# A gate moved at the head of the load queue, one pair's x turned by DMA, and the last output tile in two halves

## The chip, the cores and the metric

The kernel runs on one core of a Trainium2 chip, as one launch. The metric is device time in microseconds (us). The engines of the core are named as in the profile: PE is TensorE (PEld its weight loads), DVE is VectorE, ACT is ScalarE, POOL is GpSimd and SP is SyncE. SP computes nothing: it issues DMAs, as POOL and ACT also do.

## The reference

A recurrent attention with a decaying state feeds a two-layer network with a GELU. Inputs and output are float32.

```python
# q, k, v, alpha: (4 batches, 8 heads, 768 tokens, 48)
for t in range(S):
    state = alpha[:, :, t, :, None] * state + np.einsum('bhd,bhe->bhde', k[:, :, t], v[:, :, t])
    y[:, :, t] = np.einsum('bhd,bhde->bhe', q[:, :, t], state)
x = y.transpose(0, 2, 1, 3).reshape(3072, 384)
h = x @ w_in                                     # w_in: (384, 2048)
g = 0.5 * h * (1.0 + np.tanh(np.sqrt(2 / np.pi) * (h + 0.044715 * h * h * h)))
out = g @ w_out                                  # w_out: (2048, 384)
```

## The kernel before, in words

**Tiling.** The 768 tokens are cut into six chunks of 128, and the four batches into two halves of two. A chunk with a half is a *pair*: twelve pairs, number m = 0 to 11, two batches each. A chunk with one batch is a *unit*: 24 units, each giving one output tile of 128 x 384.

**A pair's attention.** ACT takes the logarithm of alpha (`ln`, la), PE sums it along the tokens with a triangular matrix (`cum`), ACT takes exponentials (`b`, `binv`, and `bend` for the chunk's end). DVE multiplies q by b (qp) and k by binv (kp). Both are turned so that features lie on partitions (qkT): for pairs 0 to 7 by PE transposes and copies, for pairs 8 to 11 by a DMA transpose (`turn_dma`, L402). PE multiplies the turned k and q (`at`, L424), DVE masks the result (`atm`, L431), PE multiplies by v and adds the carried state (`yps`, L470 and L473). PE also computes the pair's contribution to the state (`kv`), which DVE carries on (`st`). A copy gives x in bfloat16 (L480, on ACT or DVE).

**Turning x.** The first layer needs x with features on partitions (xT). The pairs in `TURN_X` have it turned by a DMA transpose from SP (`turn_x_dma`, L408), the others by three PE transposes for each unit (xT_ps, L487) and a copy by DVE (L491). Before, `TURN_X` holds pairs 8 to 11.

**The two layers.** For each pair, 16 groups of three matmuls of 256 columns give hT (`layer1`, L497), and ACT applies the GELU into gT (L503). For each unit, 16 matmuls of 384 columns add up acc (`layer2`, L511), in four parts of four; a copy (ot, L518) and a store from SP (L523) follow. Layer 2 of pairs 0 and 1 runs after layer 1 of both, part by part over their four units; from then on each pair's layer 2 follows its layer 1.

**The order.** A planner (`Scheduler.order`) fixes the order of the instructions of every engine when the kernel is built. It goes through the tasks with costs from `W` and takes, on the engine that is free first, the task with the best priority; buffers have to come free first (`BUFS`: four tiles for layer 1's results and acc together, tag "ff"). Layer 1 and layer 2 tasks form a stream in fixed order; where PE would idle, matmuls on zeros ("idle", `fill`, L222) are put in. On the chip each engine then runs its list strictly in that order.

**Loads.** alpha, q and k of pair 0 and alpha and q of pair 1 come in quarters of 96 KB from SP and ACT (`RINGS`). All other loads are issued by POOL in the order of `LOADS`, those that change the type (v, w_in, w_out) among them. w_in and w_out come in four parts each. The entry `gatea0` is a tiny copy on POOL that reads a tile of pair 0, so that everything behind it in POOL's queue waits until that tile has landed:

```python
LOADS = ('gatea0', 'v0', 'pk1', 'in 0', 'in 1', 'v1', 'in 2', 'in 3', 'out 0', 'out 1', '2a', ...)

elif step[:4] == "gate":
    key = step[4], int(step[5]), 3
    gate = [s.add("gate", {"POOL": 150}, n, self.wait(*key), [loads[key]])]
```

'pk1' is k of pair 1 in quarters, 'in 0' a part of w_in, '2a' the first half of pair 2's four inputs, '3' all four of pair 3.

Of the kernel before, what the change touches and what calls it, by code (L numbers as in the profile page):

```python
# [7 lines left out]
F32 = mybir.dt.float32  # L8
# [6 lines left out]
W = dict(  # L15
    ln=760, exp=720, bend=170, gelu4=510, gelu2=340, table=1290,
    cum=530, cum_packed=1500, t8=450, t4=225, attn=340, kv=170, inter=170, intra=205, tx=168, l1_4=655, l1_2=340, l2=655,
    qk2=910, qk1=500, ev8=650, ev4=350, mask=640, st=1400, st0=700, xc=520, xe=330, ot=540,
    ev8_act=960, ev4_act=520, xc_act=450, xe_act=450, ot_act=450,
    strip=2120, cast=1500, weight=2080, dma=2100, issue=1100, wissue=760, sp=100, store=2600, turn=1250, landed=2200, xbar_qk=1500, xbar_x=1000, piece=330, piece_issue=450, begin=2700, cast_0=1300, share=1200, cast_1=1900, ln_packed=1040, cold=380, fill=216, zero=1100,  # L20
)
LAT = {"SP": 0, "PE": 210, "ACT": 110, "DVE": 90, "POOL": 0}

# [113 lines left out]
class _Kernel:  # L137
# [3 lines left out]

    SPLIT = (2,)
    EARLY = (0, 1)
    LOADS = ('gatea0', 'v0', 'pk1', 'in 0', 'in 1', 'v1', 'in 2', 'in 3', 'out 0', 'out 1', '2a', 'out 2', '2b', 'out 3', '3', '4', '5', '6', '7', '8', '9', '10', '11')

    PACKED, CUM_FF, R = (0, 1), (1,), 4
    RINGS = (('a', 0, 0, 'SP'), ('a', 0, 2, 'ACT'), ('a', 0, 1, 'SP'), ('a', 0, 3, 'ACT'), ('q', 0, 0, 'SP'), ('q', 0, 2, 'ACT'), ('q', 0, 1, 'SP'), ('q', 0, 3, 'ACT'), ('k', 0, 0, 'SP'), ('k', 0, 2, 'SP'), ('k', 0, 1, 'SP'), ('k', 0, 3, 'SP'), ('a', 1, 0, 'SP'), ('a', 1, 1, 'SP'), ('a', 1, 2, 'SP'), ('a', 1, 3, 'SP'), ('q', 1, 0, 'SP'), ('q', 1, 1, 'SP'), ('q', 1, 2, 'SP'), ('q', 1, 3, 'SP'))
    TABLE = ('q', 0, 3)

    TURN_QK, TURN_X = (8, 9, 10, 11), (8, 9, 10, 11)  # L150

    EV_ACT = (0, 1, 2, 3)

# [352 lines left out]
    def layer2(self, f, c, b, part):  # L506
        def emit(e):
            if part == 0:
                f["acc", c, b] = self.tile("ff", [self.C, self.d_model], F32, "acc")
            for nt in range(part * 4, part * 4 + 4):  # L510
                self.nc.tensor.matmul(f["acc", c, b], self.gT[c % self.NG][:, nt, b * self.C:(b + 1) * self.C],  # L511
                                      self.w_out[:, nt, :], start=nt == 0, stop=nt == self.NFT - 1)
        return emit

    def result(self, f, c, b):
        def emit(e):
            f["ot", c, b] = self.tile("ot", [self.C, self.d_model], F32)
            self.copy(e)(f["ot", c, b], f.pop(("acc", c, b)))  # L518
        return emit

    def store(self, f, c, b):
        r = b * self.S + c * self.C
        return lambda e: self.nc.sync.dma_start(self.out[r:r + self.C, :], f["ot", c, b])  # L523


    def tasks(self):
        s = self.s = Scheduler(self.BUFS, self.fill, 60000)
        B, NCH = self.B, self.NCH
# [5 lines left out]
        loads, n, gate = {}, 0, []  # L534
# [20 lines left out]
        for r, m, j, e in self.RINGS:  # L555
            loads[r, m, j] = s.add("load", {e: W["piece_issue"]}, n, self.load_packed(r, *pairs[m], j), land=W["piece"] + (0 if n else W["begin"]))
            n += 1
            if (r, m, j) == self.TABLE:
                s.add("table", {"ACT": W["table"]}, n, lambda e: self.act_set(LN_EXP))
        for step in self.LOADS:  # L560
            if step[0] == "v":
                rows(int(step[1:]), "v")
            elif step[0] == "p":
                r, m = step[1], int(step[2])
# [19 lines left out]
        for m, (c, i) in enumerate(pairs):  # L584
            u, P = self.p[c, i], 100 * m
# [5 lines left out]
            for lo, hi in self.parts(m):  # L591
                n = hi - lo
                ln = s.add("ln", {"ACT": W["ln_packed" if u["packed"] else "ln"] * n // 2}, P, self.ln(u, lo, hi), rows_of("a", m, lo), LN_EXP)
                cum = s.add("cum", {"PE": W["cum_packed" if u["packed"] else "cum"] * n // 2}, P - 400, self.cum(u, lo, hi), [ln])
                x = [s.add(e, {"ACT": W[e] if e == "bend" else W["exp"] * n // 2}, P + 2 + j, self.exp(u, e, lo, hi), [cum], LN_EXP)
                     for j, e in enumerate(("b", "binv", "bend") if u["sums"] else ("b", "binv"))]
# [37 lines left out]
            for j in range(2):  # L634
                b, o = 2 * i + j, P + 10 + 3 * j
                k = kp[j]
                if u["packed"]:
                    turned = every
                elif m not in self.TURN_QK:
                    turned = []  # L640
                    for which in ("q", "k") if early else ("qk",):
                        n = 4 * len(which)
                        cost = {"DVE": W[f"ev{n}"]}
                        if m in self.EV_ACT:
                            cost["ACT"] = W[f"ev{n}_act"]
                        t1 = s.add("t", {"PE": W[f"t{n}"]}, o, self.turn(u, j, which),
                                   ([qp[j]] if "q" in which else []) + ([k] if "k" in which else []))
                        turned.append(s.add("ev", cost, o, self.turned(u, j, which), [t1]))
                        t1.take("yk", turned[-1])
                        tq.append(t1)  # L650
                        if len(tq) == 1:
                            owner = turned[0]
                at = s.add("attn", {"PE": W["attn"]}, o + 1, self.attn(u, j), turned)
                ms = [s.add("mask", {"DVE": W["mask"]}, o + 2, self.mask(u, j, h), [at]) for h in range(2)]
                if (m, j) in self.AT_FF:
                    at.take("ff", ms[0]).take("ff", ms[1])
                else:
                    at.take("ca", *ms)
                y = s.add("y", {"PE": W["intra"] + (W["inter"] if c else 0)}, P + 20 + j, self.y(u, j, c, b),
                          ms + turned + [loads["v", m, j]] + ([states[b, c - 1]] if c else []))  # L660
                xc = s.add("x", {"ACT": W["xc_act"], "DVE": W["xc"]}, P + 20 + j, self.x(u, j), [y])
                if m in self.TURN_X:
                    xe = tx = s.add("turn", {"SP": W["turn"]}, P + 22 + j, self.turn_x_dma(u, j, c, b), [xc], xbar=W["xbar_x"])
                else:
                    tx = s.add("tx", {"PE": W["tx"]}, P + 22 + j, self.turn_x(u, j), [xc])
                    xe = s.add("xe", {"DVE": W["xe"]}, P + 22 + j, self.turned_x(u, j, c, b), [tx])
                    tx.take("yk", xe)
                y.take("yk", xc)
                xc.take("x", tx)
                users += [at, y]  # L670
                ats.setdefault(m, []).append(at)
                ms[0].take("atm", y)
                xts[c, b], ys[b, c] = xe, y
                vs.append(y)
                if c < NCH - 1:
                    if u["packed"]:
                        tb = s.add("t", {"PE": W["t4"]}, P + 29 + j, self.turn_back(u, j), turned)
                        k = s.add("ev", {"DVE": W["ev4"], "ACT": W["ev4_act"]}, P + 29 + j, self.turned_back(u, j), [tb])
                        tb.take("yk", k)
                        users.append(tb)  # L680
                        backs.append(tb)
                    kv = s.add("kv", {"PE": W["kv"]}, P + 30 + j, self.kv(u, j), [k, loads["v", m, j]])
                    st = states[b, c] = s.add("st", {"DVE": W["st" if c else "st0"]}, P + 30 + j, self.carry(u, j, c, b),
                                              [kv, be[j]] + ([states[b, c - 1], ys[b, c - 1]] if c else []))
                    kv.take("yk", st)
                    vs.append(kv)
                    kvs.append(kv)
                    cs.append(st)
# [14 lines left out]


        n = 0
        f, gs, l2s = {}, {}, {}
        between = {m: [x for p in self.DECAYS.get(m, ()) for x in ends[p]] for m in range(-1, len(self.BLOCKS))}

        def layer1(m):
# [14 lines left out]
        def layer2(m):  # L724
            nonlocal n
            units = [(pairs[p][0], 2 * pairs[p][1] + j) for p in ((0, 1) if m == 0 else self.BLOCKS[m]) for j in range(2)]
            parts = range(self.NFT // 4)
            first = {}
            for u, part in ([(u, part) for part in parts for u in units] if m == 0 else [(u, part) for u in units for part in parts]):
                c, b = u  # L730
                t = s.add("l2", {"PE": W["l2"]}, 10000 + n, self.layer2(f, c, b, part),
                          gs[m if m else b // 2][4 * part:4 * part + 4] + [loads["w", "out", part]], stream=n)
                l2s.setdefault(c, []).append(t)
                n += 1
                first.setdefault(u, t)
                if part == parts[-1]:
                    ot = s.add("ot", {"DVE": W["ot"], "ACT": W["ot_act"]}, -1, self.result(f, c, b), [t])
                    first[u].take("ff", ot)
                    ot.take("ot", s.add("store", {"SP": W["sp"]}, n, self.store(f, c, b), [ot]))

        for m in range(len(self.BLOCKS)):
            layer1(m)
            if m:
                layer2(m if m > 1 else 0)
# [64 lines left out]
```

## Time and profile before

| | |
|---|---|
| median of 11 runs (range) | 186.93 us (186.58 to 189.28) |
| the profiled execution's own time | 186.84 us |
| its span, first to last instruction | 185.1 us |
| granted PE clock | 1.00 |
| busy: PE, ACT, DVE, POOL | 175.8, 135.3, 105.7, 60.5 us |
| first matmul of layer 1; of layer 2 | 18.62; 33.55 us |
| first layer 1 of pairs 7 and 8 | 122.14; 135.66 us |
| end of the last POOL load | 110.9 us |
| last copy; last store issued; landed | 181.55; 182.06; 183.91 us |

A row of the profile's groups gives the line, the engine, the operation and what it writes and reads, and behind x the number of instructions. "DMA to landing" is the time from the start of an issue until its semaphore says that all has arrived. The chain that ended last is followed back from the last instruction, at each step to what released it. In the lines of slices the span is cut into 40 equal parts of 4.6 us, and each digit is the busy share in tenths.

### The profile page before, as it was taken

What the parts mean: (1) busy time and instruction counts of PE and PEld (TensorE: products, weight loads), DVE (VectorE), ACT (ScalarE), POOL (GpSimd) and SP (SyncE); (2) the same over time, 40 slices, a digit from 0 to 9 for tenths busy, and PEclk for the clock granted to TensorE, in tenths of its full rate; (3) what the DMA queues carried; (4) which work ended last, traced back from release to release, by engine and by line L of the source; (5) the groups of instructions that cost most, each with busy time, mean ns of one, the idle gap of its engine ahead of it and who ended that gap; (6) DMA issues with size and microseconds to landing.
All of it is one profiled execution on the core that took longest, in us unless ns stands there. A gap on an engine that the chain in (4) does not pass through costs nothing.

```text
span 185.1 us, 4604 instructions
## 1 busy us (share of the span) xinstructions
PE 175.8 (95%) x1851; PEld 128.3 (69%) x1851; DVE 105.7 (57%) x235; ACT 135.3 (73%) x308; POOL 60.5 (33%) x67
## 2 busy tenths in 40 slices
PE   7867999999999999999999999999999999999992
PEld 2444878666686787787688778667687677686860
DVE  7774873055969895596499798596644615000000
ACT  3646978873888789869799759788789883491931
POOL 2977356976545755644750200000000000000000
PEclk9999999999999999999999999999999999999999
DMA  5999999999999999999999966154180280311102
GB/s 152 186 222 196 199 232 209 204 208 174 191 276 179 161 231 195 186 223 198 179 227 219 177 177 118 41 122 82 39 179 27 54 189 4 87 46 43 43 7 78
DMA packets 50229, 27.56 MB, mean 149 GB/s; under 512 B 37984, under 2 KB 47264, under 8 KB 50208
## 3 DMA queue, kind: packets, MB, share of 16 engines
q0 software_dynamic: 32096, 17.70, 69.3%
q1 hardware_dynamic: 17536, 9.18, 20.1%
q10 hardware_dynamic: 576, 0.39, 0.7%
q8 instruction: 14, 0.23, 0.6%
q14 instruction: 7, 0.06, 0.1%
HBM read 25.17 MB, written 4.72 MB: 161 GB/s over the span
## 4 chain that ended last, share of the span: by engine, by line
PE 84%; DMA 8%; ACT 3%; SPq 2%; issue 1%; DVE 0%; ACTq 0%; DVEq 0%
PE acc L511 34%; PE hT L497 31%; DMA q<-in_q_dram 6%; PE at L424 4%; PE qkT_ps L364 4%; PE yps L473 2%; PE yps L470 2%; PE cum L320 2%; PE kv L441 2%; SPq L247 2%; DMA qkT<-kp 2%; PE xT_ps L487 1%; ACT L503 1%; ACT ot L518 1%; PE cum L322 1%
## 5 line engine op out<-in xcount | busy, mean ns | idle before, releaser
L497 PE MATMUL hT<-xT,w_in 128*128 128x256 bf16 x576 | 70.5, 273 | 0.6 <-ACT gT L503 0.6
L503 ACT ACTIVATE gT<-hT 128x256 bf16<-128x256 f32 x192 | 63.4, 386 | 8.6 <-PE hT L497 8.0
L511 PE MATMUL acc<-w_out,gT 128*128 128x384 bf16 x384 | 68.9, 326 | 0.0
L497 PEld LDWEIGHTS <-w_in 128*128 128x128 bf16 x576 | 54.1, 98 | 8.2 <-issue 0.9
L511 PEld LDWEIGHTS <-gT 128*128 128x128 bf16 x384 | 35.6, 97 | 20.4
L431 DVE TENSOR_TENSOR atm<-at,ut 128x512 bf16<-128x512 f32 x48 | 31.0, 685 | 16.8 <-PE at L424 16.3
L354 DVE TENSOR_TENSOR qp<-q,b 128x768 bf16<-128x768 f32 (+1 forms) x15 | 11.8, 793 | 16.2 <-DMA w_out<-in_moe_w_out_dram 6.9
L518 ACT COPY ot<-acc 128x384 f32<-128x384 f32 x17 | 8.1, 479 | 15.2 <-PE acc L511 14.1
L235 POOL DMA_DIRECT2D v<-in_v_dram x13 | 14.6, 1121 | 8.1 <-PE xT_ps L487 2.3
L235 POOL DMA_DIRECT2D k<-in_k_dram x11 | 12.2, 1106 | 12.7 <-DVE kp L354 5.0
L343 ACT ACTIVATE b<-cum 128x768 bf16<-128x768 f32 (+1 forms) x15 | 10.1, 683 | 6.7 <-PE cum L322 2.6
L235 POOL DMA_DIRECT2D a<-in_alpha_dram x11 | 12.2, 1111 | 8.1 <-ACT gT L503 2.2
L235 POOL DMA_DIRECT2D q<-in_q_dram x11 | 12.2, 1110 | 7.4 <-DMA w_out<-in_moe_w_out_dram 1.1
L213 ACT ACT_TABLE_LOAD x9 | 11.5, 1283 | 2.8 <-issue 2.6
L458 DVE TENSOR_TENSOR st<-stmp,bend 64x192 bf16<-64x192 f32 x32 | 11.3, 353 | 1.5
L354 DVE TENSOR_TENSOR kp<-k,binv 128x768 bf16<-128x768 f32 (+1 forms) x15 | 11.7, 792 | 0.3 <-ACT b L343 0.2
L456 DVE TENSOR_TENSOR stmp<-kv,st 64x192 f32<-64x192 f32 x32 | 11.3, 352 | 0.9 <-PE kv L441 0.6
L503 ACT ACT_TABLE_LOAD x9 | 11.5, 1283 | 0.2
L480 ACT CAST x<-yps 128x384 bf16<-128x384 f32 x14 | 6.7, 481 | 6.4 <-PE yps L473 6.3
L382 DVE COPY qkT<-qkT_ps 128x1024 bf16<-128x1024 bf16 (+1 forms) x14 | 9.2, 687 | 2.5 <-PE qkT_ps L364 2.4
L222 PE MATMUL idle<-zero 128*128 128x512 bf16 x27 | 9.3, 455 | 1.2 <-DVE blk L757 1.2
L343 ACT ACTIVATE binv<-cum 128x768 bf16<-128x768 f32 (+1 forms) x15 | 10.1, 684 | 0.0
(61 smaller groups left out, 162.0 us busy)
## 6 DMA issues: line engine op xcount, KB each, us to landing
out_dram<-ot SPq DMA_DIRECT2D x24, 192.0 KB, 2.5
a<-in_alpha_dram POOLq DMA_DIRECT2D x9, 384.0 KB, 13.4
q<-in_q_dram POOLq DMA_DIRECT2D x9, 384.0 KB, 13.4
k<-in_k_dram POOLq DMA_DIRECT2D x9, 384.0 KB, 13.7
v<-in_v_dram POOLq DMA_DIRECT2D x11, 192.0 KB, 13.3
w_in<-in_moe_w_in_dram POOLq DMA_DIRECT2D x4, 384.0 KB, 10.4
w_out<-in_moe_w_out_dram POOLq DMA_DIRECT2D x4, 384.0 KB, 11.7
a<-in_alpha_dram SPq DMA_DIRECT2D x6, 96.0 KB, 3.3
```

The lines of the kernel that those rows point to most:

```text
L213: nc.scalar.add_instruction(mybir.InstLoadActFuncSet(name=nc.get_next_instruction_name(), act_func_set_id=i, engine=mybir.EngineType.Activ ...
L222: self.nc.tensor.matmul(ps, self.zero[:, 0:self.C], self.zero, start=True, stop=True)
L235: (nc.sync if e == "SP" else nc.gpsimd).dma_start(u[n][:, lo:hi].rearrange("t b h d -> t (b h) d"), src)
L343: self.nc.scalar.activation(u[n].rearrange("t i h d -> t i (h d)")[:, lo:hi], cum, AF.Exp, scale=1.0 if n == "b" else -1.0)
L354: self.nc.vector.tensor_tensor(out, rows, b, op=ALU.mult)
L431: self.nc.vector.tensor_tensor(u["atm", i][:, o], u["at", i][o], self.ut[:, None, :].to_broadcast([self.C, self.H // 2, self.C]), op=ALU.mult)
L456: nc.vector.tensor_tensor(s[ps], acc, old[ps, :, fs], op=ALU.add)
L458: nc.vector.tensor_tensor(new[ps, :, fs], acc, u["bend"][ps, i, :, None].to_broadcast([64, H // 2, D]), op=ALU.mult)
L497: self.nc.tensor.matmul(h, self.w_in[:, j, nt * self.C:(nt + 1) * self.C], self.xT[c][:, j, lo:hi].rearrange("p g t -> p (g t)"), start=j ...
L503: return lambda e: self.nc.scalar.activation(self.gT[c % self.NG][:, nt, lo * self.C:hi * self.C], f.pop(("h", c, lo, nt)), AF.Gelu_apprx_ ...
L511: self.nc.tensor.matmul(f["acc", c, b], self.gT[c % self.NG][:, nt, b * self.C:(b + 1) * self.C], self.w_out[:, nt, :], start=nt == 0, sto ...
L518: self.copy(e)(f["ot", c, b], f.pop(("acc", c, b)))
```

## The change

The first gate reads q of pair 0 instead of its alpha, and a second one, reading q of pair 1, is put ahead of w_in. Pair 7 joins `TURN_X`. (The planner gets a lateness `late_x` for such turns of pairs below 7; with pair 7 as the first in `TURN_X` it applies to none.) The last unit's second layer is computed in two halves of 192 columns, each over all sixteen blocks of features, in an accumulator tile of its own, with its own copy and its own store.

```diff
-    LOADS = ('gatea0', 'v0', 'pk1', 'in 0', 'in 1', 'v1', 'in 2', ...
+    LOADS = ('gateq0', 'v0', 'pk1', 'gateq1', 'in 0', 'in 1', 'v1', 'in 2', ...
-    TURN_QK, TURN_X = (8, 9, 10, 11), (8, 9, 10, 11)
+    TURN_QK, TURN_X = (8, 9, 10, 11), (7, 8, 9, 10, 11)
...
             if part == 0:
                 f["acc", c, b] = self.tile("ff", [self.C, self.d_model], F32, "acc")
-            for nt in range(part * 4, part * 4 + 4):
-                self.nc.tensor.matmul(f["acc", c, b], self.gT[c % self.NG][:, nt, b * self.C:(b + 1) * self.C],
-                                      self.w_out[:, nt, :], start=nt == 0, stop=nt == self.NFT - 1)
+            if part == 2 and (c, b) == (self.NCH - 1, self.B - 1):
+                f["acc", c, b] = self.tile("ff", [self.C, self.d_model], F32, "acc")
+            last, w = (c, b) == (self.NCH - 1, self.B - 1), self.d_model // 2
+            for lo, hi, nts in (((part // 2 * w, part // 2 * w + w, range(part % 2 * 8, part % 2 * 8 + 8)),) if last else
+                                ((0, self.d_model, range(part * 4, part * 4 + 4)),)):
+                for nt in nts:
+                    self.nc.tensor.matmul(f["acc", c, b][:, lo:hi], self.gT[c % self.NG][:, nt, b * self.C:(b + 1) * self.C],
+                                          self.w_out[:, nt, lo:hi], start=nt == 0, stop=nt == self.NFT - 1,
+                                          skip_group_check=last)
...
-    def result(self, f, c, b):
+    def result(self, f, c, b, half=None):
...
-    def store(self, f, c, b):
+    def store(self, f, c, b, half=None):
...
-                    xe = tx = s.add("turn", {"SP": W["turn"]}, P + 22 + j, self.turn_x_dma(u, j, c, b), [xc], xbar=W["xbar_x"])
+                    xe = tx = s.add("turn", {"SP": W["turn"]}, P + 22 + j, self.turn_x_dma(u, j, c, b), [xc], xbar=W["xbar_x"], late=W["late_x"] * (m < 7))
...
+                if (c, b) == (NCH - 1, self.B - 1):
+                    t.deps += gs[m]
...
+                    if part % 2:
+                        ot = s.add("ot", {"DVE": W["ot"], "ACT": W["ot_act"]}, -1, self.result(f, c, b, part // 2), [t])
+                        ots.append((ot, s.add("store", {"SP": W["sp"]}, n, self.store(f, c, b, part // 2), [ot])))
```

Since the planner starts anew from these, other things move in the changed program's order: at the start pair 1's cum stands ahead of pair 0's at, and pair 1's turns of k ahead of the first hT; in SP's queue pair 7's two turns stand between pair 8's q and k; pair 8's first at comes 24 matmuls of acc later and its first x moves from DVE to ACT.

More of the change, by code (lines that the diff above doesn't have):

```diff
@@ L19 @@
     ev8_act=960, ev4_act=520, xc_act=450, xe_act=450, ot_act=450,
-    strip=2120, cast=1500, weight=2080, dma=2100, issue=1100, wissue=760, sp=100, store=2600, turn=1250, landed=2200, xbar_qk=1500, xbar_x=1000, piece=330, piece_issue=450, begin=2700, cast_0=1300, share=1200, cast_1=1900, ln_packed=1040, cold=380, fill=216, zero=1100,
+    strip=2120, cast=1500, weight=2080, dma=2100, issue=1100, wissue=760, sp=100, store=2600, turn=1250, landed=2200, xbar_qk=1500, xbar_x=1000, late_x=2500, piece=330, piece_issue=450, begin=2700, cast_0=1300, share=1200, cast_1=1900, ln_packed=1040, cold=380, fill=216, zero=1100,
 )
@@ L143 @@
     EARLY = (0, 1)
-    LOADS = ('gatea0', 'v0', 'pk1', 'in 0', 'in 1', 'v1', 'in 2', 'in 3', 'out 0', 'out 1', '2a', 'out 2', '2b', 'out 3', '3', '4', '5', '6', '7', '8', '9', '10', '11')
+    LOADS = ('gateq0', 'v0', 'pk1', 'gateq1', 'in 0', 'in 1', 'v1', 'in 2', 'in 3', 'out 0', 'out 1', '2a', 'out 2', '2b', 'out 3', '3', '4', '5', '6', '7', '8', '9', '10', '11')
     PACKED, CUM_FF, R = (0, 1), (1,), 4
@@ L509, in emit @@
                 f["acc", c, b] = self.tile("ff", [self.C, self.d_model], F32, "acc")
-            for nt in range(part * 4, part * 4 + 4):
-                self.nc.tensor.matmul(f["acc", c, b], self.gT[c % self.NG][:, nt, b * self.C:(b + 1) * self.C],
-                                      self.w_out[:, nt, :], start=nt == 0, stop=nt == self.NFT - 1)
+            if part == 2 and (c, b) == (self.NCH - 1, self.B - 1):
[7 more added lines that the diff above has]
+                                          skip_group_check=last)
+            if last:
+                f["acc", c, b, part // 2] = f["acc", c, b]
         return emit
-    def result(self, f, c, b):
+    def result(self, f, c, b, half=None):
         def emit(e):
-            f["ot", c, b] = self.tile("ot", [self.C, self.d_model], F32)
-            self.copy(e)(f["ot", c, b], f.pop(("acc", c, b)))
+            if half in (None, 0):
+                f["ot", c, b] = self.tile("ot", [self.C, self.d_model], F32)
+            sl = slice(0, self.d_model) if half is None else slice(half * self.d_model // 2, (half + 1) * self.d_model // 2)
+            self.copy(e)(f["ot", c, b][:, sl], f["acc", c, b] if half is None else f["acc", c, b, half][:, sl])
         return emit
-    def store(self, f, c, b):
+    def store(self, f, c, b, half=None):
         r = b * self.S + c * self.C
-        return lambda e: self.nc.sync.dma_start(self.out[r:r + self.C, :], f["ot", c, b])
+        sl = slice(0, self.d_model) if half is None else slice(half * self.d_model // 2, (half + 1) * self.d_model // 2)
+        return lambda e: self.nc.sync.dma_start(self.out[r:r + self.C, sl], f["ot", c, b][:, sl])
     def tasks(self):
@@ L705, in tasks @@
         n = 0
-        f, gs, l2s = {}, {}, {}
+        f, gs, l2s, ots, parts_of = {}, {}, {}, [], []
         between = {m: [x for p in self.DECAYS.get(m, ()) for x in ends[p]] for m in range(-1, len(self.BLOCKS))}
@@ L735, in layer2 @@
                 first.setdefault(u, t)
-                if part == parts[-1]:
+                if (c, b) == (NCH - 1, B - 1):
+                    t.deps += gs[m]
+                    if part % 2 == 0:
+                        parts_of.append(t)
+                    if part % 2:
+                        ot = s.add("ot", {"DVE": W["ot"], "ACT": W["ot_act"]}, -1, self.result(f, c, b, part // 2), [t])
+                        ots.append((ot, s.add("store", {"SP": W["sp"]}, n, self.store(f, c, b, part // 2), [ot])))
+                        parts_of[part // 2].take("ff", ot)
+                        if part == 3:
+                            ots[0][0].take("ot", *[x[1] for x in ots])
+                elif part == parts[-1]:
                     ot = s.add("ot", {"DVE": W["ot"], "ACT": W["ot_act"]}, -1, self.result(f, c, b), [t])
```

## The prediction

> **What bounds the kernel now.** I read the page's engine shares and slices, then the chain that ended last, then single transfers in the first 35 us.
>
> ```profile
> PE 175.8 (95%) x1851; PEld 128.3 (69%) x1851; DVE 105.7 (57%) x235; ACT 135.3 (73%) x308; POOL 60.5 (33%) x67
> ...
> PE   7867999999999999999999999999999999999992
> ...
> DMA  5999999999999999999999966154180280311102
> ```
>
> TensorE (PE) is full from slice 5 (18.5 us) to slice 39. The DMA engines are full too, from slice 1 to slice 22. So a saving of PE work, or an earlier PE start, reaches the end, unless the loads cannot follow. The chain in order of time, first 36 us (start, length, what):
>
> ```profile
> 8.91 7.28 DMA q<-in_q_dram
> ...
> 16.79 0.55 DVE kp L354
> ...
> 18.78 0.33 PE hT L497 x3
> ...
> 29.13 4.59 PE hT L497 x42
> 33.72 2.44 PE acc L511 x15
> ```
>
> Before 18 us the chain waits for the last quarter of pair 1's q, issued at 8.91 and landed 7.28 us later, at 16.2. Pair 0's quarters landed in 3.5 to 3.9 us. The first layer's PE work (hT) starts at 18.62, the second layer's (acc) at 33.55.
>
> The third and fourth parts of w_in, by their issues (issue time in the row, then time to landing):
>
> ```profile
> L262 POOL DMA_DIRECT2D w_in<-in_moe_w_in_dram x1: 738/738/738, 12.4 to 12.4; - x1
> ...
> DMA to landing us min/median/max: 10.3/10.3/10.3
> ...
> L262 POOL DMA_DIRECT2D w_in<-in_moe_w_in_dram x1: 767/767/767, 13.2 to 13.2; - x1
> ...
> DMA to landing us min/median/max: 11.5/11.5/11.5
> ```
>
> They land at 22.8 and 24.7. By the timeline, PE reaches the groups of hT that need them at 23.0 and 25.0: 0.2 and 0.3 us later. This is the second limit, just behind the first, and the chain does not show it.
>
> The end of the chain, then the ot tile's last three copies and stores:
>
> ```profile
> 176.32 5.21 PE acc L511 x32
> 181.53 0.02 issue
> 181.55 0.48 ACT ot L518
> ...
> L523 SPq DMA_DIRECT2D out_dram<-ot x3: 332/332/332, 171.6 to 182.1; - x3
> ...
> DMA to landing us min/median/max: 1.9/1.9/1.9
> ```
>
> After the last matmul come a copy of 0.48 us and a store of 1.85 us (its packets take 0.68 us of that), in series.
>
> **What the Trainium skill says.** (1) "DMA: Bandwidth & Descriptors", section "Queues, rings and completion order": each DMA engine takes turns between the queue rows that have work, packet by packet. The trace agrees: pair 1's pieces landed about 0.4 us apart before the first POOL transfer moved packets (7.14 us), then 0.3 to 2.1 us apart. (2) "TensorE: Matmul & The Clock Gate", section "Wait — 56ns, not 53.3ns?": one matmul every N / 2.4 GHz + 2.5 ns. The trace agrees: 384 columns every 162.6 ns, 256 every 109. (3) "ScalarE: Activation LUTs", section "What ACT_TABLE_LOAD costs": 186 + 0.833 N ns for an activation. The trace has 478 ns for the 384-column copy; the formula gives 506. I use the slope only.
>
> **Part 1, the gates: +0.4 us.** Today POOL's gate waits for alpha of pair 0 (4.16), and v of pair 0 is issued at 4.93. The new first gate waits for q of pair 0, landed at 6.01: 1.85 us later, so v's issue is at 6.8 and its first packets at 9.0. The four k pieces of pair 1 stand behind it in POOL's queue. Then a second gate waits for q of pair 1; behind that stand all of w_in and w_out, v of pair 1 and every later load.
>
> *When q of pair 1 lands.* From 7.1 to 9.0 the SP queue now has the DMA engines alone. At the 205 to 220 KB/us of 5 to 7 us it gains 0.2 MB, so at 9.0 about 355 KB of the 1.97 MB on the SP and ACT queues are left. Beside v's packets that queue moved 77, 139 and 106 KB in the three microseconds from 7 us on. So 355 KB need 3.3 us: 12.4, and 0.6 to 1.2 us more for the engine that finishes last (today its packets thin out at 15.0 and it lands at 16.2). I take 13.2: 3 us earlier than now. Pair 1's qp, kp, transposes and pair 0's x then let hT start at about 16.7.
>
> *When the weights land.* From landing to POOL's issue takes 0.77 us (4.16 to 4.93), from issue to first packet 2.2 us for v (1.28 of it issue), so 1.7 for w_in (0.76 issue): first packets at 15.7. v and k of pair 1 are through by about 15.0, so the DMA engines rest for about 0.7 us. A part of w_in takes 1.95 us (24.68 to 26.68 and its neighbours): the first lands at 17.65 against 16.96. It sets the start of hT: 17.7 against 18.62.
>
> *Where that gain goes.* From there PE would reach the third part's groups at about 21.8, and it isn't there. Today the second part and v of pair 1 took 3.95 us together, 0.6 more than their own 1.95 and 1.36; some of that I give back, so the third and fourth parts land at about 23.3 and 25.2, 0.5 later than now. PE waits some 1.5 us. After the third part landed, today, 10.77 us passed to the first acc; in the changed order of PE a few things (a turn of k, a fill) stand earlier and I count 10.65. First acc: 33.95 instead of 33.55, **+0.4 us**. The later loads shift alike; pair 2's second half (alpha landed 34.7, used 35.9) and pair 3's alpha (landed 40.9, used 41.0, but PE asks for its cum at 45.5) have the room; from pair 4 on there are 9 us (landed 48.7, used 57.9).
>
> Bounds. Below: the queues cost each other 0.9 us today from 7.1 to 17 us (9.8 us for 8.95 us of work at the rates above); were all of it regained, the weights land 0.4 us earlier: −0.5. Above: q of pair 1 gets only a third of the engines beside v, as its landings (8.1 to 16.2 us for 2.9 us of pieces) can be read, lands at 14.3, and the weights come 1.6 to 1.8 us later: +1.5 to +1.7.
>
> **Part 2, pair 7's x: −0.35 us.** Six PE transposes go, at 57 ns each (0.34 us), and two DVE copies of 0.35 us, which lie beside other work: DVE is 57% busy. PE is full there (110 to 116 us). Added on SP: two transposes by DMA, 1.18 us of issue and 1.1 to 2.3 us to landing each. In SP's queue they stand between pair 8's q and k:
>
> ```profile
> 110.54 1.33 SPq L402 DMA_TRANSPOSE qkT<-qp  x1
> 112.57 1.24 SPq L402 DMA_TRANSPOSE qkT<-kp  x1
> ```
>
> x of pair 7 is copied by 111.2 and 113.1, so k of pair 8 is issued at 114.3 and lands at 117.4, 1.8 us later than now. Pair 8's at, which waits for it, is planned behind 24 more matmuls of acc (3.9 us), at about 120.5. xT is needed at 122.1 and is there by 116. The following x of pair 8 moves from DVE to ACT inside the gelus (0.48 us more on ACT) and is needed at 135.5; I find it landed by 132. So cost nothing, cover 3 us or more; bounds −0.4 and +0.3 (ACT's backlog delaying the next table load, where PE's cum has 0.5 us).
>
> **Part 3, the last unit by halves: −0.4 us.** 16 matmuls of 384 columns become 32 of 192: 32 × 82.5 − 16 × 162.6 = +0.04 us; weight loads double, but pass in 25 to 57 ns elsewhere. The first half is copied and stored beside the second half's 1.32 us. After the last matmul the copy is half as wide: 192 × 0.833 = −0.16 us. The last store moves half, its packets 0.34 us instead of 0.68: −0.3. Sum −0.4; bounds −0.5 and −0.1 (if a store's time does not shrink).
>
> **Sum.** +0.4 − 0.35 − 0.4 = −0.35 us. The profiled execution took 186.84 us (span 185.1 and 1.7 around it), 0.09 under the median of the 11 runs. 186.84 − 0.35 = **186.5 us**.
>
> **Rivals.** *A, the front gains (−1.2 us, 185.6).* The weights land 0.4 us earlier, since the queues no longer hinder each other; the front gives −0.5, the rest −0.75. For it: the 0.9 us lost today, and the chain's 7.28 us on q. Against it: the engines must rest while the gate opens. *B, the gate opens late (+0.75 to +0.95, 187.6 to 187.8).* One mechanism: v and k of pair 1 still take two thirds of the engines from q of pair 1, w_in starts after 16.5, and PE waits for its third part. It outweighs the other parts once the third part lands more than 0.9 us later than today's 22.8. For it: POOL's strict order behind the gate, and 0.2 us of room today. Against: 2 us of free engines from 7 to 9 us. *C, the crossbar or the replanned order stalls PE (+0.3 instead of −0.35, 187.1).* *D, the gate does not hold what it should:* only if POOL's queue had later work ready ahead of it, which its order excludes.
>
> **Numbers.** Forecast 0.50, A 0.30, B 0.15, C 0.05, D nil. 0.5% is 0.93 us, about what a measurement of this kernel tells from no change. A is past it (0.28), as is an edge of the forecast (0.02): faster 0.30. B with less from parts 2 and 3 (0.06), C's worst (0.03) and the forecast's other edge (0.02): slower 0.11. The rest, 0.59, is the same. Range 185.4 (A with part 3 at its bound) to 187.7 (most of B).
>
> **What would show it.** Right: q of pair 1 lands near 13, the first w_in near 17.7, hT starts before 18 and then waits around 22 to 23 for w_in, first acc near 34; no xT_ps on PE after pair 6; the last copy 0.32 us and the last store 1.55 us. Wrong: first acc before 33.2 or after 34.8, a PE gap between 110 and 136, or a last store as long as now.

## The result, and the profile after

The changed kernel takes 188.49 us (median of 12 runs, 187.98 to 189.75). Against the kernel before, timed beside it on the same chip, that is 1.0078 times as long [1.0057, 1.0100]: **slower by 0.78%**, some 1.5 us, where I had forecast no measurable change. It lies above the range that I gave (185.4 to 187.7). The profiled execution took 188.67 us with a span of 186.9, 1.8 more than the span before.

From the page of the changed kernel, the same parts as shown of before (one digit for each 4.7 us; PEclk is the granted PE clock in tenths), and the row of the first layer's matmuls, which ends with the idle time before them and what ended most of it:

```profile
PE 177.4 (95%) x1860; PEld 130.2 (70%) x1860; DVE 104.5 (56%) x232; ACT 136.1 (73%) x310; POOL 61.1 (33%) x68
...
PE   7895799999999999999999999999999999999993
...
PEclk9999699999999999999999999999999999999999
DMA  5895999999999999999999997745263181311102
...
L497 PE MATMUL hT<-xT,w_in 128*128 128x256 bf16 x576 | 71.2, 275 | 3.5 <-DMA w_in<-in_moe_w_in_dram 3.1
```

The last of these rows on the page of the kernel before:

```profile
L497 PE MATMUL hT<-xT,w_in 128*128 128x256 bf16 x576 | 70.5, 273 | 0.6 <-ACT gT L503 0.6
```

Two rows have a hole in the same place: slice 3 (14.0 to 18.7 us) is 5 for DMA, where before it was 9, and 5 for PE, where it was 7; slice 4 is 7 for PE instead of 9. The PE waits 3.1 us for w_in. In slice 4 it ran part of the time at a lower clock (PEclk 6). From slice 5 on PE is as full as before.

The chain that ended last, its first 40 us (start, length, what):

```profile
8.61 5.43 DMA q<-in_q_dram
...
14.19 0.58 POOL gate L255
14.76 1.45 POOL w_in L262 x2
16.21 1.16 POOL v L235
17.38 0.72 POOL w_in L262
18.10 9.07 DMA w_in<-in_moe_w_in_dram
27.17 0.28 issue
27.45 11.48 DMA a<-in_alpha_dram
```

Before, this chain went from q of pair 1 through the attention to the first layer. Now it goes from q of pair 1 through the new gate into POOL's queue, and stays with the loads until pair 2's alpha has landed at 38.93. The front of the kernel is bound by POOL's loads and their order.

Busy time of each engine in stretches of 2 us (PE, PEld, DVE, ACT, POOL, each with its number of instructions), the last three columns being the PE clock, the share of the DMA engines and GB/s, both counted by the starts of packets:

```profile
14.00:16.00 2.00, 1.86 (x23) 1.16 (x23) 1.92 (x6) 1.19 (x3) 1.81 (x3) 1.00 0.00 0
16.00:18.00 2.00, 0.86 (x10) 0.53 (x8) 1.41 (x3) 1.44 (x3) 2.00 (x3) 1.00 0.90 113
18.00:20.00 2.00, 0.05 (x1) 0.05 (x2) 0.00 (x0) 0.56 (x1) 2.00 (x4) 0.88 1.11 167
20.00:22.00 2.00, 2.00 (x14) 1.63 (x15) 0.12 (x1) 0.77 (x2) 2.00 (x3) 0.50 1.78 174
```

and the first of these stretches before:

```profile
14.00:16.00 2.00, 1.89 (x32) 1.18 (x29) 0.00 (x0) 2.00 (x7) 2.00 (x3) 1.00 1.23 212
```

From 14 to 16 us next to nothing is moved, where the kernel before moved 212 GB/s. For two more microseconds the DMA engines are slow, and from 18 to 20 us PE and DVE stand all but still, while ACT only ends the loading of a table (0.56 us). When PE starts, its clock is granted at half (0.50).

The four parts of w_in in the changed kernel, by two of their issues (issue time in the row, then time to landing):

```profile
L262 POOL DMA_DIRECT2D w_in<-in_moe_w_in_dram x1: 753/753/753, 14.7 to 14.7; - x1
...
DMA to landing us min/median/max: 5.2/5.2/5.2
...
L262 POOL DMA_DIRECT2D w_in<-in_moe_w_in_dram x1: 741/741/741, 17.4 to 17.4; - x1
...
DMA to landing us min/median/max: 7.9/7.9/7.9
```

The first part, issued 14.71, lands at 19.91 (16.96 before); the second at 21.92, the third at 25.30 (22.78), the fourth at 27.17 (24.68). The first layer starts at 19.95 and the second at 36.34, 2.8 us later than before.

The end of the chain:

```profile
178.68 5.25 PE acc L516 x48
183.96 0.32 ACT ot L528
```

and the copies and stores of output tiles from 170 us on, with least, median and longest time in ns:

```profile
L528 ACT COPY ot<-acc x5: 319/479/480, 170.9 to 184.0; 128x384 f32<-128x384 f32 x3, 128x192 f32<-128x192 f32 x2
L534 SPq DMA_DIRECT2D out_dram<-ot x5: 332/332/332, 171.4 to 184.3; - x5
...
DMA to landing us min/median/max: 1.6/1.9/1.9
```

Here the change did what it says: the last copy takes 0.32 instead of 0.48 us, the last store 1.61 instead of 1.85.

Set side by side, the starts of stages give the balance of the two profiled executions: second layer +2.79 us; first layer of pair 6 +3.08; of pair 8 +2.42; of pair 11 +2.37; end +1.82. So the front lost 2.8 and then 0.3 us, pairs 6 and 7 won back 0.66, and pair 11 with the tail 0.55.

### The profile page after: what moved, and what is told of

Same layout as the page of the kernel before. It is cut to its first block, busy times and chain, and to the rows that moved or that the text cites. A ratio compares the mean times of both kernels' runs of the same rounds, so it can differ in the third digit from the quotient of the medians.

```text
span 186.9 us, 4621 instructions
## 1 busy us (share of the span) xinstructions
PE 177.4 (95%) x1860; PEld 130.2 (70%) x1860; DVE 104.5 (56%) x232; ACT 136.1 (73%) x310; POOL 61.1 (33%) x68
## 4 chain that ended last, share of the span: by engine, by line
PE 74%; DMA 18%; POOL 2%; SPq 2%; ACT 2%; issue 1%; ACTq 0%; POOLq 0%
PE acc L516 32%; PE hT L497 26%; DMA a<-in_alpha_dram 6%; DMA q<-in_q_dram 5%; DMA w_in<-in_moe_w_in_dram 5%; PE at L424 4%; PE qkT_ps L364 3%; PE yps L473 2%; PE yps L470 2%; PE cum L320 2%; DMA qkT<-kp 2%; SPq L247 2%; PE kv L441 2%; POOL w_in L262 1%; PE xT_ps L487 1%; ACT L503 1%
## 5 line engine op out<-in xcount | busy, mean ns | idle before, releaser
L516 PE MATMUL acc<-w_out,gT 128*128 128x384 bf16 (+1 forms) x400 | 68.8, 319 | 0.0
L516 PEld LDWEIGHTS <-gT 128*128 128x128 bf16 x400 | 36.8, 97 | 19.6
L431 DVE TENSOR_TENSOR atm<-at,ut 128x512 bf16<-128x512 f32 x48 | 31.0, 685 | 16.1 <-PE at L424 15.6
L354 DVE TENSOR_TENSOR qp<-q,b 128x768 bf16<-128x768 f32 (+1 forms) x15 | 11.8, 793 | 17.7 <-ACT b L343 10.3
L528 ACT COPY ot<-acc 128x384 f32<-128x384 f32 (+1 forms) x18 | 8.3, 462 | 13.9 <-PE acc L516 12.7
L382 DVE COPY qkT<-qkT_ps 128x1024 bf16<-128x1024 bf16 (+1 forms) x13 | 8.7, 688 | 6.7 <-PE qkT_ps L364 6.6
L480 ACT CAST x<-yps 128x384 bf16<-128x384 f32 x15 | 7.2, 479 | 6.2 <-PE yps L473 6.1
## 6 DMA issues: line engine op xcount, KB each, us to landing
a<-in_alpha_dram POOLq DMA_DIRECT2D x9, 384.0 KB, 13.2
```

Source lines behind the costliest of these rows:

```text
L354: self.nc.vector.tensor_tensor(out, rows, b, op=ALU.mult)
L382: self.copy(e)(t, ps)
L431: self.nc.vector.tensor_tensor(u["atm", i][:, o], u["at", i][o], self.ut[:, None, :].to_broadcast([self.C, self.H // 2, self.C]), op=ALU.mult)
L516: self.nc.tensor.matmul(f["acc", c, b][:, lo:hi], self.gT[c % self.NG][:, nt, b * self.C:(b + 1) * self.C], self.w_out[:, nt, lo:hi], star ...
```

## The experiments

Theory: the second gate costs, since it keeps the weights out of POOL's queue until q of pair 1 is in, and the queue then has to start from empty; the other two parts gain. Rivals, as they are called in the expectations: R1, the halved PE clock is the main loss; R2, the first gate delays v and with it the rest; R3, the crossbar or the halves cost something. Each kernel was timed in five rounds beside the kernel before, and ratios are to that. The runs of the kernel before spread (186.0 to 190.6 us over all rounds) and their median lies above its profiled execution, and ratios of single parts do not multiply up to that of the whole change: both gates, the crossbar and the halves alone give 1.0121 × 0.9923 × 0.9944 = 0.999, where the whole is 1.0078. I have no shown cause for that. In the profiles the parts come nearer to the whole: gates_only ends 3.58 us later than the kernel before and no_gates 1.31 earlier, together +2.27, and the changed kernel +1.82. One more thing is needed to read single profiles. The kernel before, no_gates, turn_only and halves_only have the same order of loads, and of the work of ACT and DVE, at the start, yet their second layers start at 33.55, 33.59, 33.84 and 32.98 us: differences of under 0.9 us between two fronts are not resolved by one profile each. I take signs from ratios and sizes from stretches of the profiles.

### The second gate

**Both gates alone** (`gates_only`): the changed kernel with `TURN_X` of before and the last unit whole.

```diff
-    TURN_QK, TURN_X = (8, 9, 10, 11), (7, 8, 9, 10, 11)
+    TURN_QK, TURN_X = (8, 9, 10, 11), (8, 9, 10, 11)
...
-            last, w = (c, b) == (self.NCH - 1, self.B - 1), self.d_model // 2
+            last, w = False, self.d_model // 2
...
```

> Only the two gates of the change; pair 7's x and the last unit as before. Theory (the second gate leaves the DMA engines empty and the weights land 2.5 us late): first layer-2 matmul at 36.3 us as in the changed kernel, about +2.6 us over before (ratio near 1.014), because the crossbar and the halves, which are undone here, had given 1.1 us back. Rival R3 (the gates cost nothing in the end, the crossbar turn and the halves are what is slow): no slower than before.

Measured: 189.62 us, ratio 1.0121 [1.0076, 1.0167]. First part of w_in at 20.18, second layer at 36.52: the front loss of the whole change, and more.

**Neither gate** (`no_gates`): the changed kernel with the head of the load queue as before, so the crossbar and the halves alone.

```diff
-    LOADS = ('gateq0', 'v0', 'pk1', 'gateq1', 'in 0', 'in 1', ...
+    LOADS = ('gatea0', 'v0', 'pk1', 'in 0', 'in 1', ...
```

> The changed kernel with the gate of before (alpha of pair 0, no second gate): pair 7's x by DMA and the last unit by halves alone. Theory: first layer-2 matmul at 33.5 as before, and -1.1 us over the whole (-0.7 between 108 and 122 us, -0.4 to -0.5 at the end), ratio near 0.994. Rival R3: slower than before by 1 us or more.

Measured: 185.80 us, ratio 0.9908 [0.9878, 0.9939]. Second layer at 33.59, as before (33.55). So the loss belongs to the gates, and the rest of the change is a gain.

**The first gate moved, no second one** (`q0_only`):

```diff
-    LOADS = ('gateq0', 'v0', 'pk1', 'gateq1', 'in 0', 'in 1', ...
+    LOADS = ('gateq0', 'v0', 'pk1', 'in 0', 'in 1', ...
```

> The changed kernel without its second gate; the first gate still reads q of pair 0. v of pair 0 is issued at 6.7 us as in the changed kernel, but the weights follow k of pair 1 at once. Theory: the DMA queue of POOL never runs empty, w_in part 1 lands by 17 to 17.5, first layer-2 matmul near 33.5 (33.2 to 34), total -0.8 to -1.3 us against before. Rival R2 (the first gate, by making v of pair 0 and k of pair 1 1.8 us later, is what costs): still about +1.2 us as the changed kernel.

**The first gate as before, with the second one** (`a0_q1`):

```diff
-    LOADS = ('gateq0', 'v0', 'pk1', 'gateq1', 'in 0', 'in 1', ...
+    LOADS = ('gatea0', 'v0', 'pk1', 'gateq1', 'in 0', 'in 1', ...
```

> The changed kernel with the first gate back on alpha of pair 0 (v of pair 0 issued at 4.9), the second gate on q of pair 1 kept. Theory: q of pair 1 now shares with v and k and lands at 14.3 to 15, the second gate opens no earlier than in the changed kernel, w_in part 1 lands at 20 to 21, first layer-2 matmul 36.3 to 37, total +1.2 to +2 us. Rival R2: -1.1 us, as without any gate.

Measured: q0_only 185.04 us, ratio 0.9884 [0.9838, 0.9930]; a0_q1 189.66 us, ratio 1.0112 [1.0069, 1.0156]. The second gate decides the sign, whichever first gate stands before it. Both runs went further than I expected: q0_only gained some 2 us (2.04 in its profile) where I expected 0.8 to 1.3, and in a0_q1, where q of pair 1 landed at 15.46 instead of 14.3 to 15, the second layer started at 38.72 instead of 36.3 to 37. A replanned start is not what costs either: up to 60 us ACT and DVE run the same list in q0_only and in the changed kernel. The chain of q0_only, with the same columns as above:

```profile
6.26 0.18 POOL gate L255
...
6.81 6.81 DMA v<-in_v_dram
...
13.91 8.32 DMA w_in<-in_moe_w_in_dram
22.23 0.05 issue
22.28 0.83 PE hT L497 x6
...
33.03 2.60 PE acc L516 x16
```

and two of its stretches:

```profile
14.00:16.00 2.00, 1.65 (x24) 1.07 (x22) 1.36 (x4) 1.12 (x3) 2.00 (x3) 1.00 1.26 211
16.00:18.00 2.00, 1.99 (x22) 1.46 (x20) 1.99 (x5) 1.44 (x3) 2.00 (x4) 1.00 1.66 178
```

In the same 14 to 16 us in which the changed kernel moved nothing, this one moves 211 GB/s. The third part of w_in lands at 22.23 and still bounds the front (PE waits 0.7 us for it), and the second layer starts at 32.87: 3.5 us before the changed kernel's. It is also 0.7 us before that of no_gates, but only 0.1 before that of halves_only, which has the old head of the queue. What the second gate was put there to protect needed none: q of pair 1 lands at 13.91 without it, at 14.04 with it. It is the first gate that brings q forward, from 15.6 to 16.5 in the four profiles with the old head of the queue to 13.9. Whether that makes q0_only faster than no_gates the times can't say, since their intervals overlap.

**A second gate that opens early** (`q1_first`): the gate reads 32 partitions, hence only the first of q's quarters.

```diff
-        return lambda e: self.nc.gpsimd.tensor_copy(self.gate[:, 0:1], u[r][:, 0, 0, 0:1])
+        return lambda e: self.nc.gpsimd.tensor_copy(self.gate[0:32 if m else self.C, 0:1], u[r][0:32 if m else self.C, 0, 0, 0:1])
```

> The changed kernel, but the second gate reads 32 partitions, so it waits only for the first quarter of q of pair 1 (landed at 10.2 in the changed kernel) instead of the last (14.0). Theory: the gate opens as POOL reaches it (10.2 to 10.7 us), the DMA engines have no gap, w_in part 1 lands near 17, first layer-2 matmul 33 to 33.8, total -0.8 to -1.3 us against before. If the order of loads itself were at fault (k of pair 1 and v ahead, whatever the gap), it would stay at +1 us.

**A second gate on three quarters** (`q1_three`): the same with 96 for 32.

> The changed kernel with the second gate on three quarters of q of pair 1 (partitions 0 to 95), which land about 1 us before the last. It puts a point between the gate on one quarter and on all. Theory: w_in part 1 lands 5.2 us after its issue, whenever that is; issue at 13.7, landing at 18.9, first layer-2 matmul near 35.2, ratio 1.000 to 1.004. By the prediction's terms (3.65 us from issue to landing in an empty queue) it would land at 17.4 and layer 2 start at 33.7.

Measured: q1_first 185.14 us, ratio 0.9875 [0.9829, 0.9922]; q1_three 187.84 us, ratio 1.0065 [1.0044, 1.0087]. The gates of q1_first, first and last start:

```profile
L255 POOL COPY gate<-q x2: 186/192/197, 6.3 to 10.4; 128x1 f32<-128x1 f32 x1, 32x1 f32<-32x1 f32 x1
```

The same two gates with the second at 10.4 instead of 14.2 cost nothing (second layer at 32.82): it is not an instruction more on POOL that hurts but the time at which it lets go. Of q1_three I had wanted a point between, with the gate open a little earlier. In its profile q came later than I assumed and the weights were issued at 14.70, as in the changed kernel (14.71); so it is rather a repeat of that, without its low clock; its first part of w_in took 5.06 us from issue to landing, near the 5.2 that I had written.

**The gate behind two parts of w_in** (`late_gate`):

```diff
-    LOADS = ('gateq0', 'v0', 'pk1', 'gateq1', 'in 0', 'in 1', 'v1', ...
+    LOADS = ('gateq0', 'v0', 'pk1', 'in 0', 'in 1', 'gateq1', 'v1', ...
```

> The changed kernel with its second gate two places further back: after parts 1 and 2 of w_in instead of ahead of them. POOL still waits for the whole of q of pair 1, and all other loads still stand behind that. Theory (what costs is that nothing is queued for the DMA engines while POOL waits): the two parts of w_in, 3.9 us of transfers, cover the wait; no gap in POOL's packets, w_in part 1 lands near 16.8, part 4 within 0.5 us of the kernel without the second gate (24.1), first layer-2 matmul 32.7 to 33.4, ratio near 0.988. Rival G (any wait of POOL for q of pair 1 delays the later weights by its length): part 4 lands at 26 or later, first layer-2 matmul at 35 or later, ratio 1.000 or more.

Measured: 186.35 us, ratio 0.9972 [0.9944, 1.0000]. The third part of w_in by its issue:

```profile
L262 POOL DMA_DIRECT2D w_in<-in_moe_w_in_dram x1: 741/741/741, 15.0 to 15.0; - x1
...
DMA to landing us min/median/max: 7.9/7.9/7.9
```

With two parts of w_in queued, the DMA engines have work while the gate waits: the longest pause between the queue's packets is 0.05 us, against 2.17. The second layer starts at 33.74, so 2.6 of the 3.5 us between the changed kernel and q0_only are gone. The other 0.9 stays, and neither number that I had written was met. The third and fourth parts land 0.7 and 1.2 us later than in q0_only. Two things differ there: v of pair 1 is issued 2.05 us later (13.83 against 11.78), and POOL's queue then moves 126 to 179 GB/s in the microseconds from 18 to 25 us, against 168 to 207. What each of them costs, and why the queue moves less, is not shown.

### The clock

**Twelve idle matmuls ahead of the first hT** (`warm`), to keep PE busy in part of the wait:

```diff
+            if (c, lo, nt) == (0, 0, 0):
+                self.fill(12)(e)
```

> The changed kernel with 12 more matmuls on zeros (2.6 us) on PE just ahead of the first group of layer 1, inside the 3.3 us in which PE waits for w_in. No result changes. Rival R1 (the cost is the TensorE clock, which was granted at half for 3.4 us after that wait): the clock stays at 1.0, the first groups run in 0.33 us each, and 1.0 to 1.7 us of the loss goes (ratio to before near 1.000). Theory (PE waits for the third and fourth part of w_in in any case): first layer-2 matmul moves by less than 0.4 us, ratio near 1.006.

The change itself was run once more beside it, later and on one chip with a repeat of warm.

> The changed kernel itself, for the comparison with warm_again on the same chip in the same rounds. Both theories: 188.0 to 188.9 us, ratio near 1.008.

> The changed kernel with the 12 matmuls on zeros again, beside the changed kernel itself. Theory (the half clock costs only what PE loses before it waits for part 3 anyhow, 0.2 to 0.5 us): 0.2 to 0.5 us under after_again. Rival R1 (the clock is the main loss): 1.0 us or more under it.

Measured: warm 188.00 us, ratio 1.0041 [1.0012, 1.0070]; on the second occasion warm_again 188.07 us, ratio 1.0071 [1.0052, 1.0090], and after_again 188.10 us, ratio 1.0091 [1.0057, 1.0124]. Side by side there is no difference to see: the medians are 0.03 us apart and the intervals overlap, so neither my 0.2 to 0.5 us nor R1's 1.0 appears. The first profile of warm had its second layer at 34.95, 1.4 us before the changed kernel's, where I had allowed 0.4; but its q of pair 1 landed 0.9 us earlier as well (13.13) and its weights with it (18.96), and warm_again starts its second layer at 35.69, after_again at 35.63. The clock row on after_again's page:

```profile
PEclk9999999999999999999999999999999999999999
```

and what its PE waited for from 16 to 50 us (us in total, times, longest):

```profile
PE hT L497 <- DMA w_in<-in_moe_w_in_dram: 3.1, 2, 1.8
PE cum L320 <- ACT la L303: 0.4, 1, 0.4
```

The same program, at full clock throughout, waits the same 3.1 us, now in two pieces (first and third part). Its loss is there all the same, as it is in the six of the changed kernel's twelve runs that were at full clock (median 188.47 us, where the kernel before has 186.93). The halved clock comes in some executions and not in others. In the profiled one it cost some 0.4 us, by an estimate from the time between the fourth part of w_in and the second layer (9.17 us, against 8.79 in after_again). It is not the cause: R1 falls.

### The other two parts alone

These two edits are shown against the kernel before.

**Pair 7's x through the crossbar** (`turn_only`):

```diff
-    TURN_QK, TURN_X = (8, 9, 10, 11), (8, 9, 10, 11)
+    TURN_QK, TURN_X = (8, 9, 10, 11), (7, 8, 9, 10, 11)
```

> Before with pair 7's x by DMA transpose alone. Prediction's term: -0.35 us (six PE transposes). The profile of the changed kernel shows -0.7 us between the first layer 1 of pairs 6 and 8; then ratio 0.996 to 0.998. A stall by the DMA queue would show as 0 or slower.

**The last unit in halves** (`halves_only`): all else as before.

```diff
+            last, w = (c, b) == (self.NCH - 1, self.B - 1), self.d_model // 2
+            for lo, hi, nts in (((part // 2 * w, part // 2 * w + w, range(part % 2 * 8, part % 2 * 8 + 8)),) if last else
...
```

> Before with the last unit's second layer by halves alone. Prediction's term: -0.4 us (copy 0.16, store 0.3, PE +0.04), ratio near 0.998; last copy 0.32 us, last store 1.55 us. If a store's time does not shrink with its size: -0.1 us.

Measured: turn_only 185.72 us, ratio 0.9923 [0.9895, 0.9950]; halves_only 186.57 us, ratio 0.9944 [0.9917, 0.9972]. Both gain, by their ratios more than expected; how much of that the profiles bear out is worked out below. The transposes of turn_only from 95 to 130 us,

```profile
L487 PE MATMUL xT_ps<-ident,x x6: 216/218/219, 101.2 to 102.7; 128*128 128x128 bf16 x6
```

with, from 100 to 130 us of the kernel before,

```profile
L487 PE MATMUL xT_ps<-ident,x x12: 216/219/219, 100.9 to 113.3; 128*128 128x128 bf16 x12
```

and of halves_only

```profile
L528 ACT COPY ot<-acc x3: 319/319/480, 178.5 to 181.1; 128x192 f32<-128x192 f32 x2, 128x384 f32<-128x384 f32 x1
...
DMA to landing us min/median/max: 1.6/1.6/1.9
```

In turn_only there are no transposes of x after pair 6's six; the kernel before has six further ones up to 113.3. From pair 6's first layer to pair 8's it takes 27.04 us in turn_only, 27.70 before.

## Why the prediction was wrong, point by point

**Part 1, where it failed: the time of a load from POOL's issue to its landing when the queue starts empty.** The sum had q of pair 1 at 13.2, 0.77 us to POOL's issue, 1.7 to the first packets and 1.95 for the part, hence w_in's first part at 17.65, some 3.7 us after its issue. In the profile:

| term | predicted | measured |
|---|---|---|
| q of pair 1 lands | 13.2 | 14.04 |
| to the issue of w_in | 0.77 | 0.67 |
| issue to landing, first part | 3.7 | 5.20 |
| to the third part | 5.65 | 5.39 |
| third part to the second layer | 10.65 | 11.04 (10.64 at full clock) |
| second layer starts | 33.95 | 36.34 |

The third row is the largest miss, and it repeats: 5.03 to 5.21 us in the seven profiles with a gate between pk1 and the weights that waits for at least three quarters of q. The first packets came 1.5 us after the issue (predicted 1.7). But from there to its landing the part took 3.7 us instead of 1.95: from 16 to 17 us the DMA engines moved 40 GB/s, in the next three microseconds 185, 150 and 184, and only then 198. The parts behind it follow at the distances that I had counted (2.01, 1.38, 2.00 and 1.87 us). I had priced a part by its neighbours in a full queue; such a distance, from landing to landing, holds neither the start of the stream nor the time from a load's last packets to its semaphore. The Trainium skill, "DMA: Bandwidth & Descriptors", section "Anatomy of one DMA — SWDGE (gpsimd) path", gives about 2.0 us fixed plus the bytes over 436 GB/s. For a part of w_in, 0.39 MB as written or 0.79 as read, that makes an estimate of 2.9 to 3.8 us; the 5.0 to 5.2 measured here are above both, so it would not have saved the sum. Whether the thin start comes from the emptied queue, the cast or the two loads issued right behind it no run separates.

The landing of q, 0.84 us later than predicted, is the second miss. It varied between 13.1 and 14.7 us in the runs with q of pair 0 as the first gate, so 13.2 was its good end. Where the second gate ahead of the weights opened late, POOL's queue then rested 0.9 to 2.2 us in those runs, not 0.7.

**The same part, "the later loads have the room".** This failed as well, by less. Pair 2's second-half alpha landed 4.2 us later (38.93) and PE's cum waited: 0.3 us more in the changed kernel, 0.5 in after_again. I had added one shift to all loads; by this one it had grown from 2.5 to 4.2. By the bytes that POOL's queue had moved, added up from the DMA records, it did not grow: the queue reached each total from 1.1 to 6.2 MB 3.6 to 3.8 us later than before, from the first weights on. The landings of w_in had hidden a part of that. When its fourth part landed, the queue had moved 2.51 MB in all, against 2.74 before: less of the loads behind it had gone ahead. At the landing of this alpha the totals are nearly alike (4.96 and 4.88 MB), and the whole delay shows.

**Rival B** had the place and the sign: the gate opens late and PE waits for w_in. Its mechanism (v and k take the engines from q of pair 1, w_in after 16.5) is not what happened: w_in's first packets came at 16.2, and the rest of the loss lay behind them. Its price, up to 187.8, was short by the start-up. My upper bound for part 1, +1.5 to +1.7, left it out too: 2.8 were lost there. Rival A's thought, that the queues no longer hinder each other, has little in it: with the first gate moved q of pair 1 lands some 2 us earlier, but by its bytes POOL's queue in q0_only is only 0.1 to 0.2 us ahead of the kernel before, where A had the weights 0.4 us earlier; and the earlier second layer of q0_only lies nearly within the spread of single profiles.

**The place of the wait.** I expected PE to start at 17.7 and wait at 22 to 23. In the profiled execution all 3.1 us came ahead of the first matmul, and behind the half clock no second wait was left; at full clock (after_again) it is two waits, as described but longer.

**Part 2, right in sign, too small:** −0.66 us between the first layers of pairs 6 and 8 instead of −0.35. The six transposes are half of it (6 × 55 ns, as predicted). Another 0.22 comes with hT (0.18 of it a wait for a GELU that is gone) and 0.11 with acc; the replanned order of PE's work may account for both, which no run separates. The cover of SP's queue held: no stall of pair 8 is in the trace, and rival C did not come.

**Part 3, right in size and kind:** from the start of the last matmul to the end 3.88 us before, 3.22 in no_gates. Copy −0.16 as predicted, store −0.24 (predicted −0.3), the narrower last matmul −0.08, −0.18 after the landing. The matmuls before it took 0.12 longer (predicted 0.04). That is −0.54 against −0.4. The last matmul is a term that I had not counted; most of the time after the landing is not the halves' doing, since turn_only, which stores its last tile whole, has 0.13 of it too. In halves_only, where it is 0.06, the same sum gives −0.43.

**Rival D** fell: the trace has v's issue behind the first gate and the weights behind the second.

**A misreading ahead of the sum.** The landings about 0.4 us apart before POOL's first packets (7.14) are those of pair 0's q and k (0.2 to 0.6 us apart). None of pair 1's pieces had landed by then; the first came at 8.09. That SP's pieces landed further apart once POOL's queue moved, up to 2.1 us, stands.

So two of three parts gained what they should or more, 1.2 us together in the profile, and the gates took 3.1 at the front instead of 0.4.

## What to carry to other kernels

When a gate holds back a load queue, count the restart: the price of a load in a full queue is its distance from its neighbour, the price of the first one after a pause is its whole time from issue to landing, here 5.0 to 5.2 instead of 1.95 us. Ask whether the transfer to be protected is hindered at all, and let the gate open while earlier transfers still fill the engines: the version without the second gate, or with one that opens at 10.4 us, beats both kernels (ratios 0.9884 [0.9838, 0.9930] and 0.9875 [0.9829, 0.9922]), though with the old gate the other two parts alone come to 0.9908 [0.9878, 0.9939], so that what the moved first gate adds is not shown. And when later loads are said to have room, take their delay from the bytes by which the queue is behind, not from the first landings, which showed 2.5 us of 3.6 to 3.8 here.

## What was not expected of the hardware

In the profiled execution PE's clock was granted at half from 19.51 to 22.92 us, for 3.41 us. PE's matmuls on both sides of that moment:

```profile
16.25 0.61 PE L364 MATMUL qkT_ps<-ident,kp 128*128 128x128 bf16 x8
...
19.95 1.46 PE L497 MATMUL hT<-xT,w_in 128*128 128x256 bf16 x6 [3.10 <-DMA w_in<-in_moe_w_in_dram]
```

The Trainium skill, "TensorE: Matmul & The Clock Gate", section "Part 1: The HAM clock gate", says that PE falls to half clock after an idle window of about 3.4 us, and that the phase of the windows is free. The trace agrees on the length and the phase: the stretch at full clock before the fall is 13.65 us, four times 3.41, and in the profiles here the first full clock begins anywhere from 4.7 to 7.0 us. It does not agree that the window has to be idle. The clock fell 2.65 us after PE's last matmul (16.86), while PE still waited, and in the 3.41 us before the fall PE was busy for 0.76. In gates_only it was busy for 0.94 us of the 3.41 before its fall, in a0_q1 for 1.70, and there the half clock lasted 6.83 us. So a pause shorter than the window was enough. How little work is too little the runs do not say: after_again kept its clock with 1.58 us of work in its emptiest such window between 10 and 34 us.

Six of the twelve runs of the changed kernel have the mean clock of the profiled one (0.991 instead of 1.00), with nearly the same median: 188.70 against 188.47 us. At full clock (after_again) PE waits for the third part of w_in instead, so that part of what the slow stretch costs would have been waiting anyway.
